# One fused H3-mixer and token-MLP kernel on one core: seven filler matmuls fewer before the last inverse stage, ScalarE's gelu table loaded after the inverse evictions, and new due times for its planner

## The chip, the core and the metric

The kernel runs on one core of one Trainium2 chip. The metric is the device time of one execution in microseconds (us). Below, PE is TensorE (matmuls; "PEld" its weight loads), DVE is VectorE, ACT is ScalarE, POOL is GpSimd, SP is SyncE, whose queue here only starts transfers.

## The reference

All inputs are bfloat16; the batch is 1, S = 2048 rows, D = 448 channels, F = 1792.

```python
x  = A_q
# mixer: short convolution of k, times v, long convolution by FFT, gate with the normed x
ks = sum over t of shift(k, t) * shift_k[:, t]          # 4 taps
kv = ks * v
y  = irfft(rfft(kv, 2S) * rfft(ssm_k, 2S))[:S] + kv * ssm_D
h  = x + layernorm(x) * y
# token MLP, over the rows
u  = gelu(einsum("sd,sf->df", layernorm(layernorm(h)), w1) + b1)   # tanh form
out = h + (einsum("df,fs->ds", u, w2) + b2).T
```

## The kernel before

The row index of every tensor is split as s = 16q + r, with q on the 128 partitions and r in 16 columns of tiles of 128 x 448 elements. All of SBUF is one tensor "arena" and all of PSUM is one tensor "ps" with 8 banks, so the profile knows only these two names and stages are told apart by line.

The convolution is a Fourier transform in two matmul stages with a transposing shuffle between them, done for the kernel (tag "k", with the filter) and for kv (tag "u"):

- **emit_tables** makes the sine tables and the small stage matrices, with Sin on ACT. It ends with a one-element gelu (line 793) whose only purpose is that its table load happens there.
- **emit_kv** (lines 868 to 890): DVE multiplies four shifted rows of k by the taps (879), PE adds them with an identity (885), DVE multiplies by v (888). **emit_kT** transposes the filter (914).
- **emit_stage1** (928 to 951), for k and then u: two matmuls for each r (933), an eviction by ACT alone (943), and two shuffle transfers, of 112 partitions from POOL and 16 from SP (947), into TK or TU. The evicted tile lies in a ring of 8 slots until both have landed. Every later tile needs all 16 shuffles of its tag.
- **emit_stage2** (956 to 971): four pairs of half-width matmuls (964) and an eviction by ACT or DVE for each of 16 tiles i. Tiles of k are scaled on the way out (653 on ACT, 656 on DVE), tiles of u are not (652, 655).
- **emit_ct** (973 to 1001): POOL copies (985, 990), PE transposes (996) and evictions make ET, the table of the last stage.
- **emit_products_i1** (1005 to 1055): DVE forms the products of a u tile and a k tile (1015), PE applies the first inverse stage (1027), ACT or DVE evicts in pairs, and shuffles go into TZ (1051; for the last pair 1040, from POOL, SP and ACT).
- **emit_warm** (1057 to 1062): matmuls whose result nobody reads, into one bank. N_WZ of them follow the last first-stage matmul; N_WI and N_WJ more lie inside the last inverse stage.
- **emit_q** (1072 to 1093): mean and variance of the rows of x, on DVE (1083, 1085) and POOL (1088, 1091).
- **emit_i2** (1102 to 1182): the last inverse stage, two matmuls for each r (1118), a gate by ACT with Identity (1125), the combination with x on DVE (1132), a sum of squares on ACT (1148) or bn_stats on DVE, small steps on POOL (1155 to 1167), and the normed row Q (1173).
- **emit_mlp** (1212 to 1250): the first layer for seven column blocks as rows of Q come (1218), gelu on ACT (1208), seven more blocks (1228), the second layer (1238), the final addition on DVE (1242), output on SP.

No order is written out by hand. Every operation is entered with a **due time** (`sch.t0`), its data dependencies, and a set of engines that may do it. `_Sched.schedule` then simulates the engines with estimated durations: an engine that is free takes, among the operations that are ready, the one with the smallest due time. Due times hold nothing back; they only rank what is ready at the same moment. An operation that ACT or DVE may do (most evictions) is passed over by DVE as long as ACT is due to be free within `flex_slack` ns, unless two or more operations are waiting for ACT (lines 329 to 332). The order found is emitted as one in-order stream for each engine, with semaphore waits where a dependency crosses engines.

The due times are set by constants on lines 639 to 645: T_U1 + T_DU1 r for stage 1 of u; T_K2 + T_D2 i and T_U2 + T_D2 i for stage 2 of k and of u; T_I1 + T_DI1 i for the products and first inverse stage; T_CT for ET's transposes; T_BIAS for a small transpose of b1; T_Q + T_DQ g for the statistics of rows 2g and 2g + 1; T_I2 + T_DI2 r for the last inverse stage, T_M1 + T_DI2 r for the MLP's first layer; and T_I2 - 50 for the N_WZ fillers.

Of the kernel before, what the change touches and what calls it, by code (L numbers as in the profile page):

```python
# [6 lines left out]
ACT = mybir.ActivationFunctionType  # L7
# [91 lines left out]
class _Sched:  # L99
# [48 lines left out]
    def op(self, W, fn, r=(), w=(), br=(), bw=(), n=0, kind=None, est=None, dmab=None, keng=16, rate=None, after=(), safter=()):  # L148
        o = _Op()
        o.id = len(self.ops)  # L150
        o.engs = W if isinstance(W, tuple) else (W,)
        o.eng = None
        o.fn = fn
        o.is_dma = dmab is not None
        o.nbytes = dmab or 0
        o.keng = keng
        o.lat = 2000.0 + o.nbytes / (22.0 * keng) if o.is_dma else 70.0
        if o.is_dma:
            o.est = {e: (600.0 if e != "pool" else 820.0) for e in o.engs}
        elif est is not None:  # L160
            o.est = dict(est) if isinstance(est, dict) else {e: est for e in o.engs}
        else:
            o.est = {e: self.est_of(e, n, kind) for e in o.engs}
        o.ev = None
        o.t0 = self.t0
        o.rate = rate or (18.0 if keng == 8 else 26.0)
        o.tag = self.tag
        o.acq = []
        o.bufs = []
        o.extra = []  # L170
        preds = set(after)
        spreds = set(safter)
        for spec in r:
            for c in self._cells(spec):
                preds.update(c.w)
                c.r.append(o.id)
        for spec in w:
            g = spec[2] if len(spec) > 2 else None
            for c in self._cells(spec):
                rd = [x for x in c.r if x != o.id]  # L180
                if g is not None and c.g == g and not rd:
                    preds.update(c.gb)
                    c.w.append(o.id)
                else:
                    base = rd if rd else list(c.w)
                    preds.update(base)
                    c.w = [o.id]
                    c.r = []
                    c.g = g
                    c.gb = base  # L190
        for b in br:
            if len(self.ops) and all(self.ops[x].engs == ("pe",) for x in b.writers):
                preds.add(b.writers[-1])
            else:
                preds.update(b.writers)
            b.readers.append(o.id)
            o.bufs.append(b)
            b.users.append(o.id)
        for b in bw:
            if not b.writers:  # L200
                o.acq.append(b)
            else:
                spreds.add(b.writers[-1])
            b.writers.append(o.id)
            o.bufs.append(b)
            b.users.append(o.id)
        preds.discard(o.id)
        spreds -= preds
        o.preds = sorted(preds)
        o.spreds = sorted(spreds)  # L210
        self.ops.append(o)
        return o.id
# [22 lines left out]
            return 300.0 + 0.9 * n  # L235
        return 450.0

    flex_slack = 600.0
    flex_back = 2

    def backlog(self, ready, ops, started, ready_t, t):
# [268 lines left out]
def _build(nc, A_q, A_k, A_v, A_shift_k, A_ssm_k, A_ssm_D, B_w1, B_b1, B_w2, B_b2, out):  # L510
# [8 lines left out]
    R = 16  # L519
# [37 lines left out]
    o_JK = o_DR + 896  # L557
# [8 lines left out]
    with ctx:  # L566
        sch = _Sched(nc, ctx, n_dma_sems=112, small_off=SMALL)
# [63 lines left out]
        def Ppair(b):  # L631
            s0, s1 = b.slots
            return PS[:, s0:s1 + 1, 0:D]
# [3 lines left out]

        FX = ("act", "dve")
        T_KV, T_DKV, T_KT, T_K1, T_DK1, T_U1, T_DU1 = -37.75, 0.96, -26.42, -39.56, 0.44, 2.72, 0.9
        T_K2, T_U2, T_D2, T_CT, T_BIAS, T_I1, T_DI1 = 29.29, -14.6, 1.375, 22.37, 56.3, 7.01, 0.974  # L640
        T_Q, T_DQ, T_I2, T_DI2, T_M1, T_W1 = 83.98, 14.35, 85.76, 0.401, 102.98, 122.45

        T_TH, T_TN = -36.0, -30.0
        T_CP, T_XL, T_WB = 20.0, -35.53, 154.44
        N_WZ, N_WI, N_W0, N_WK, N_WJ = 34, 6, 9, 3, 8

        def evac(dst, src, w, b, n, scale=None, engs=FX, r=(), est=None):

# [8 lines left out]
            bs = [b] if b is not None else []  # L657
            return op(engs, fn, r=r, w=w, br=bs, n=n, kind="psum", est=est)


        def emit_tables():
            N8 = 8192.0
# [124 lines left out]
            for k, (dst, i) in enumerate(((FW, 0), (MA, 1), (MB, 1))):  # L787
# [2 lines left out]
                   r=[(o_sv + 512 * k, 512), (o_msk + 512 * i, 512)], w=[(o_BD + 256 * k, 256)], n=128, kind="1x")  # L790
            op("pool", lambda e, W: e.tensor_scalar(out=MN, in0=MA, scalar1=-1.0, scalar2=None, op0=ALU.mult),
               r=[(o_BD + 256, 256)], w=[(o_BD + 768, 256)], n=128)
            op("act", lambda e, W: e.activation(out=JK[:, 0:1], in_=bias[:, 1:2], func=ACT.Gelu_apprx_tanh),
               r=[(o_b + 4, 4), (o_sv, 4 * NB)], w=[(o_JK, 4)], n=1)

        r_E = lambda r: (o_E + 512 * r, 512)
        r_ET = lambda r: (o_ET + 512 * r, 512)
# [203 lines left out]
                     est={"act": 1020.0, "dve": 690.0})  # L1001

        i1_last = []

        def emit_products_i1():
            for jj in range(R // 2):
                ms = []
                for h in range(2):
                    i = 2 * jj + h
                    sch.t0 = T_I1 + T_DI1 * i  # L1010
                    m = _Buf(mring)
                    ms.append(m)
                    ru = (o_TU + i * 2 * DB, 2 * DB)
                    aft = [x for w in wbufs for x in w.readers] if i == 0 else [mfirst[0]]
                    op("dve", lambda e, W, m=m, i=i: e.tensor_tensor(  # L1015
                        out=MR(m.slots[0]).rearrange("p (x y) d -> p x y d", x=2),
                        in0=TU[:, i].unsqueeze(2).broadcast_to([128, 2, 2, D]),
                        in1=TK[:, i].unsqueeze(1).broadcast_to([128, 2, 2, D]), op=ALU.mult),
                       r=[ru, (o_TK + i * 2 * DB, 2 * DB)], bw=[m], n=4 * D, after=aft)
                    if i == 0:  # L1020
                        mfirst.append(len(sch.ops) - 1)
                bs = [_Buf(psum, 2) for _ in range(2)]
                for h in range(2):
                    for t, (tab, xy) in enumerate(((MA, 0), (MN, 3), (MB, 1), (MB, 2))):
                        for par in range(2):
                            P = slice(64 * par, 64 * par + 64)
                            k = op("pe", lambda e, W, b=bs[h], m=ms[h], par=par, t=t, tab=tab, xy=xy, P=P: e.matmul(  # L1027
                                Pb(b, par), tab[P, :], MR(m.slots[0])[P, xy, :], start=(t == 0), stop=(t == 3)),
                               r=r_iv, br=[ms[h]], bw=[bs[h]], n=D, est=D / 4.15)
                            i1_last.append(k)  # L1030
                    evac(lambda jj=jj, h=h: TU[:, 2 * jj:2 * jj + 2, h, :], lambda b=bs[h]: Ppair(b),
                         [(o_TU + (4 * jj + h) * DB, DB), (o_TU + (4 * jj + 2 + h) * DB, DB)], bs[h], 2 * D)
                if jj == R // 2 - 1:
                    for h in range(2):
                        for par in range(2):
                            j = 2 * jj + par
                            p0 = 64 * (j & 1) + 32 * ((j >> 1) & 1) + (j >> 2)
                            o_h = o_TU + (2 * j + h) * DB
                            for q_, a, b_, j0 in (("sp" if h and par else "pool", 0, 112, 0), ("act" if h else "sp", 112, 128, 14)):
                                k = op(q_, lambda e, W, j=j, h=h, p0=p0, a=a, b_=b_, j0=j0: e.dma_start(  # L1040
                                    TZ[p0:p0 + 29:4, j0:j0 + (b_ - a) // 8, h, :], TU[a:b_, j, h, :]),
                                       r=[(o_h, DB)], w=[(o_TZ + j0 * 2 * DB, (b_ - a) // 8 * 2 * DB, "zpool" if a == 0 else "zsp")],
                                       dmab=(b_ - a) * DB, keng=8)
                                if a == 0:
                                    shuf["zpool"] = k
                    continue
                for par in range(2):
                    j = 2 * jj + par
                    p0 = 64 * (j & 1) + 32 * ((j >> 1) & 1) + (j >> 2)
                    for q_, a, b_, j0 in (("pool", 0, 112, 0), ("sp", 112, 128, 14)):  # L1050
                        shuf["z" + q_ + str(j)] = shuf["z" + q_] = op(q_, lambda e, W, j=j, p0=p0, a=a, b_=b_, j0=j0: e.dma_start(  # L1051
                            TZ[p0:p0 + 29:4, j0:j0 + (b_ - a) // 8].rearrange("p r c d -> p r (c d)"),
                            TU[a:b_, j].rearrange("p c d -> p (c d)")),
                           r=[(o_TU + j * 2 * DB, 2 * DB)], w=[(o_TZ + j0 * 2 * DB, (b_ - a) // 8 * 2 * DB, "z" + q_)],
                           dmab=(b_ - a) * 2 * DB, keng=8)
# [44 lines left out]
        qs = view(o_qst, [R, 4], f32)  # L1100

        def emit_i2():
            sch.t0 = T_M1 + 30.0
            op("pool", lambda e, W: e.tensor_tensor(out=bm, in0=qs[:, :, 0], in1=b2c, op=ALU.add),
               r=[(o_qst, 256), (o_b2c, 64)], w=[(o_bm, 64)], n=16)
# [192 lines left out]
```

## Time and profile before

| | us |
|---|---|
| five runs | 188.37, 188.92, 191.35, 191.58, 191.84 |
| their median | 191.35 |
| the profiled execution | 188.37 |
| its span, first to last instruction | 186.6 |
| busy in the span: PE / DVE / ACT / POOL | 173.8 / 110.0 / 97.2 / 71.4 |
| matmuls of 1218, 1228, 1238 (MLP), summed | 23.0, 21.4, 42.5 |
| the 48 filler matmuls of 1061 | 9.6 |
| ACT table loads: line 699 and line 793 | 1.3 and 1.3 |

The profiled execution is the lowest of the five runs. Its span is divided into the front (tables, kv, stages 1 and 2, products), which ends with the last eviction of the first inverse stage at 82.0 us; the shuffles after it, until about 87.4; the last inverse stage, which overlaps the first layer of the MLP, until 120; and two stretches of MLP matmuls to the end. A line of a timeline gives start, duration, engine, line of the source, operation and the number of instructions that it merges; in brackets is how long the engine had been idle before and what ended that.

### The profile page before, as it was taken

The page shows a single profiled execution, that of the slowest core. Times are in us where ns is not written, and L with a number is a line of the kernel's source. Part 1 is how long each engine was busy: PE and PEld are TensorE (multiplying, and loading weights), DVE is VectorE, ACT ScalarE, POOL GpSimd, SP SyncE. Part 2 cuts the span into 40 slices and gives each one's busy share as a digit, 9 for nine tenths or more (in the row PEclk, how much of TensorE's full clock was granted, in tenths as well). Part 3 has the DMA queues.
Part 4 walks back from the last instruction along what each step waited for, and adds up shares of the span by engine and source line. Part 5 has one row for each costly group of instructions (what it writes and reads, how often), then busy time and mean ns, then how long its engine had stood idle before and what let it go on. Part 6 is the DMA issues. An engine that isn't in the chain of part 4 may idle for free.

```text
span 186.6 us, 2835 instructions
## 1 busy us (share of the span) xinstructions
PE 173.8 (93%) x1033; PEld 91.8 (49%) x1033; DVE 110.0 (59%) x181; ACT 97.2 (52%) x141; POOL 71.4 (38%) x177
## 2 busy tenths in 40 slices
PE   7998897898988989899989999999999999999993
PEld 2653342343432433245334545555557777777772
DVE  8877999787789999997979756000001122212221
ACT  3497989888889989951886483442121000000000
POOL 8946976699520044587278576000000000000000
PEclk9999999999999999999999999999999999999999
DMA  5999597778449916774999999800000100111111
GB/s 167 377 418 316 181 260 222 233 222 236 137 115 393 353 46 183 225 238 112 351 394 401 425 422 422 343 5 0 0 0 4 49 34 15 49 53 49 49 49 49
DMA packets 15893, 35.44 MB, mean 190 GB/s; under 512 B 3901, under 2 KB 10062, under 8 KB 15878
## 3 DMA queue, kind: packets, MB, share of 16 engines
q1 hardware_dynamic: 11222, 25.66, 36.7%
q0 software_dynamic: 4608, 9.56, 17.9%
q8 instruction: 8, 0.13, 0.3%
q14 instruction: 7, 0.06, 0.1%
q10 hardware_dynamic: 48, 0.03, 0.0%
HBM read 22.37 MB, written 1.84 MB: 130 GB/s over the span
## 4 chain that ended last, share of the span: by engine, by line
PE 78%; ACT 10%; DVE 7%; DMA 3%; issue 1%; ACTq 0%
PE ps L1238 23%; PE ps L1228 11%; PE ps L1218 10%; PE ps L1061 5%; PE ps L885 5%; PE ps L1027 5%; ACT arena L943 4%; ACT arena L652 4%; PE ps L964 4%; PE ps L1118 3%; DMA arena<-arena 3%; PE ps L914 3%; PE ps L904 3%; PE ps L933 3%; DVE arena L1015 2%
## 5 line engine op out<-in xcount | busy, mean ns | idle before, releaser
L1242 DVE SCALAR_TENSOR_TENSOR arena<-ps,arena 128x448 bf16<-128x448 f32 x16 | 10.9, 684 | 56.9 <-PE ps L1238 56.9
L1238 PE MATMUL ps<-arena 128*128 128x448 bf16 x224 | 42.5, 352 | 0.0
L1238 PEld LDWEIGHTS ps<-arena 128*128 128x128 bf16 x224 | 32.3, 144 | 10.1
L943 ACT CAST arena<-ps 128x896 bf16<-128x896 f32 x32 | 26.7, 931 | 3.6 <-PE ps L933 1.7
L652 ACT CAST arena<-ps 128x896 bf16<-128x896 f32 (+1 forms) x26 | 22.0, 909 | 2.6 <-PE ps L868 1.7
L1218 PE MATMUL ps<-arena 128*128 128x448 bf16 x112 | 23.0, 353 | 0.3 <-DVE arena L1173 0.2
L947 POOL DMA_DIRECT2D arena<-arena x32 | 19.2, 601 | 7.7 <-ACT arena L943 4.7
L1228 PE MATMUL ps<-arena 128*128 128x448 bf16 x112 | 21.4, 352 | 0.0
L1208 ACT ACTIVATE arena<-ps,arena 128x448 bf16<-128x448 f32 x14 | 8.2, 639 | 20.1 <-PE ps L1228 14.7
L879 DVE TENSOR_TENSOR arena<-arena 128x1792 bf16<-128x1792 bf16 x16 | 18.2, 1175 | 0.0
L964 PE MATMUL ps<-arena 128*64 128x448 bf16 x128 | 16.4, 361 | 1.8 <-ACT arena L652 1.0
L1125 ACT ACTIVATE arena<-ps,arena 128x448 f32<-128x448 f32 x16 | 11.2, 722 | 12.0 <-PE ps L1118 9.0
L933 PE MATMUL ps<-arena 128*128 128x448 bf16 x64 | 16.0, 355 | 1.3 <-ACT arena L943 1.3
L885 PE MATMUL ps<-arena 128*128 128x448 bf16 x64 | 14.5, 354 | 2.4 <-ACT arena L943 1.8
L1015 DVE TENSOR_TENSOR arena<-arena 128x1792 bf16<-128x1792 bf16 x16 | 16.4, 1082 | 0.0
L1218 PEld LDWEIGHTS ps<-arena 128*128 128x128 bf16 x112 | 10.9, 98 | 11.1 <-DVE arena L1173 1.3
L1051 POOL DMA_DIRECT2D arena<-arena x14 | 8.2, 588 | 20.8 <-PE ps L964 15.6
L1228 PEld LDWEIGHTS ps<-arena 128*128 128x128 bf16 x112 | 11.0, 98 | 10.2
L1027 PE MATMUL ps<-arena 64*128 64x448 bf16 x128 | 14.1, 351 | 1.3 <-DVE arena L1015 0.6
L1132 DVE SCALAR_TENSOR_TENSOR arena<-arena 128x448 f32<-128x448 bf16 x16 | 10.7, 676 | 4.4 <-ACT arena L1125 4.4
L655 DVE CAST arena<-ps 128x896 bf16<-128x896 f32 (+2 forms) x11 | 9.5, 874 | 2.7 <-PE ps L868 1.2
L964 PEld LDWEIGHTS ps<-arena 128*64 128x64 f16 x128 | 5.4, 108 | 11.5 <-ACT arena L652 4.6
(88 smaller groups left out, 200.2 us busy)
## 6 DMA issues: line engine op xcount, KB each, us to landing
arena<-arena POOLq DMA_DIRECT2D x46, 196.0 KB, 4.9
arena<-in_B_w_dram SPq DMA_DIRECT2D x8, 896.0 KB, 9.2
arena<-in_B_w_dram SPq DMA_DIRECT2D x2, 2048.0 KB, 17.8
arena<-in_B_w_dram SPq DMA_DIRECT2D x2, 1536.0 KB, 19.9
arena<-in_A_k_dram SPq DMA_DIRECT2D x4, 448.0 KB, 7.8
arena<-in_A_v_dram SPq DMA_DIRECT2D x4, 448.0 KB, 8.4
arena<-in_A_q_dram SPq DMA_DIRECT2D x4, 448.0 KB, 5.0
out_dram<-arena SPq DMA_DIRECT2D x7, 224.0 KB, 1.9
```

The source lines that it names most:

```text
L652: return e.copy(out=dst(), in_=src())
L879: op("dve", lambda e, W, T=T, i=i, r=r: e.tensor_tensor(out=T[:, i], in0=KH[:, r:r + 4, :], in1=WT, op=ALU.mult), r=[(o_KH + r * DB, 4 * D ...
L885: op("pe", lambda e, W, b=b, T=T, i=i, j=j: e.matmul(Pb(b, i), ID, T[:, i, j, :], start=(j == 0), stop=(j == 3)), r=[(o_ID, 256), (o + (i ...
L933: op("pe", lambda e, W, b=b, r=r, h=h, dl=dl: e.matmul(Pb(b, h), E[:, 2 * r + h, :], src[:, r, :], start=True, stop=not dl), r=[r_E(r), (o ...
L943: return e.copy(out=dst, in_=Ppair(b)) if W == "act" else e.tensor_copy(out=dst, in_=Ppair(b))
L947: shuf[tag + q_ + str(r)] = shuf[tag + q_] = op(q_, lambda e, W, w=w, p0=p0, a=a, b_=b_, j0=j0: e.dma_start(T[p0:p0 + 29:4, j0:j0 + (b_ - ...
L964: op("pe", lambda e, W, b=bs[h], h=h, j=j, c=c, par=par: e.matmul(PS[64 * par:64 * par + 64, b.slots[c], 0:D], FW[:, 64 * c:64 * c + 64], ...
L1015: op("dve", lambda e, W, m=m, i=i: e.tensor_tensor(out=MR(m.slots[0]).rearrange("p (x y) d -> p x y d", x=2), in0=TU[:, i].unsqueeze(2).br ...
L1027: k = op("pe", lambda e, W, b=bs[h], m=ms[h], par=par, t=t, tab=tab, xy=xy, P=P: e.matmul(Pb(b, par), tab[P, :], MR(m.slots[0])[P, xy, :], ...
L1218: op("pe", lambda e, W, r=r, fc=fc, b=bs[fc]: e.matmul(Pb(b), W1A[:, r, 128 * fc:128 * fc + 128], Q[:, r, :], start=(r == 0), stop=(r == R ...
L1228: op("pe", lambda e, W, r=r, fc=fc, b=b: e.matmul(Pb(b), W1B[:, r, 128 * (fc - n0):128 * (fc - n0) + 128], Q[:, r, :], start=(r == 0), sto ...
L1238: op("pe", lambda e, W, r=r, fc=fc, b=b: e.matmul(Pb(b), W2[fc // 7][:, fc % 7, r:S:R], G[:, fc, :], start=(fc == 0), stop=(fc == NFC - 1) ...
```

## The change

The last fillers go from 34 to 27 (N_WZ). The one-element gelu leaves the tables and is entered at the head of emit_i2, with due time T_I2 - 8; it now waits for the last matmul and for the last two evictions of the first inverse stage, and its estimate is 1500 ns in place of some 231. The planner's `flex_slack` goes from 600 to 800 ns, and nine constants of due times change. No other instruction is added or removed; what else differs in the streams is their order, and which of ACT and DVE does a flexible eviction.

```diff
-    flex_slack = 600.0
+    flex_slack = 800.0
...
-        T_K2, T_U2, T_D2, T_CT, T_BIAS, T_I1, T_DI1 = 29.29, -14.6, 1.375, 22.37, 56.3, 7.01, 0.974
-        T_Q, T_DQ, T_I2, T_DI2, T_M1, T_W1 = 83.98, 14.35, 85.76, 0.401, 102.98, 122.45
+        T_K2, T_U2, T_D2, T_CT, T_BIAS, T_I1, T_DI1 = 37.66, -20.88, 1.238, 44.69, 51.65, -8.07, 0.974
+        T_Q, T_DQ, T_I2, T_DI2, T_M1, T_W1 = 84.58, 17.938, 100.42, 0.401, 102.98, 122.45
...
-        N_WZ, N_WI, N_W0, N_WK, N_WJ = 34, 6, 9, 3, 8
+        N_WZ, N_WI, N_W0, N_WK, N_WJ = 27, 6, 9, 3, 8
...
-            op("act", lambda e, W: e.activation(out=JK[:, 0:1], in_=bias[:, 1:2], func=ACT.Gelu_apprx_tanh),
-               r=[(o_b + 4, 4), (o_sv, 4 * NB)], w=[(o_JK, 4)], n=1)
+            tb_.append((bias, o_b))
...
         i1_last = []
+        i1_ev = []
...
-                    evac(lambda jj=jj, h=h: TU[:, 2 * jj:2 * jj + 2, h, :], lambda b=bs[h]: Ppair(b),
+                    k = evac(lambda jj=jj, h=h: TU[:, 2 * jj:2 * jj + 2, h, :], lambda b=bs[h]: Ppair(b),
                          [(o_TU + (4 * jj + h) * DB, DB), (o_TU + (4 * jj + 2 + h) * DB, DB)], bs[h], 2 * D)
+                    if jj == R // 2 - 1:
+                        i1_ev.append(k)
...
         def emit_i2():
+            sch.t0 = T_I2 - 8.0
+            bias, o_b = tb_[0]
+            op("act", lambda e, W: e.activation(out=JK[:, 0:1], in_=bias[:, 1:2], func=ACT.Gelu_apprx_tanh),
+               r=[(o_b + 4, 4)], w=[(o_JK, 4)], est=1500.0, after=i1_last[-1:] + i1_ev)
```

More of the change, by code (lines that the diff above doesn't have):

```diff
@@ L658, in evac @@
             return op(engs, fn, r=r, w=w, br=bs, n=n, kind="psum", est=est)
+        tb_ = []
         def emit_tables():
```

## The prediction, made before the changed kernel was built or run

> **What bounds the kernel now.** I read first the page's table of the span in 40 slices (4.67 us each; the digit is the busy share in tenths):
>
> ```profile
> PE   7998897898988989899989999999999999999993
> DVE  8877999787789999997979756000001122212221
> ACT  3497989888889989951886483442121000000000
> PEclk9999999999999999999999999999999999999999
> ```
>
> From slice 25 on only PE is full, at full clock. Up to slice 17 no engine is free: ACT and DVE share the evictions and are both full. The chain of waits gives the tail: MLP matmuls run without a gap from 112.00 to 183.69, and the change touches none of them. So the time is the moment at which the last inverse stage (line 1118) can start, plus some 99 us behind it (186.6 - 87.6).
>
> What sets that moment is read from the busy time by stretch (start:end and length, then busy us of PE, PEld, DVE, ACT and POOL, each with its number of instructions):
>
> ```profile
> 50.10:55.00 4.90, 4.41 (x42) 1.72 (x39) 4.09 (x4) 4.39 (x6) 2.15 (x9) 1.00 0.34 98
> 55.00:63.00 8.00, 6.93 (x60) 2.27 (x61) 7.14 (x8) 7.66 (x10) 0.00 (x0) 1.00 1.01 367
> 63.00:82.00 19.00, 17.36 (x157) 6.98 (x154) 18.32 (x23) 17.73 (x21) 8.70 (x15) 1.00 0.62 184
> 82.00:87.50 5.50, 5.50 (x31) 2.84 (x29) 5.37 (x17) 0.00 (x0) 5.34 (x13) 1.00 0.58 169
> ```
>
> From 55 to 82 ACT is busy 25.4 of 27.0 us and DVE 25.5: evictions and products bound this part, not PE. In the 5.5 us after it ACT does no work at all. Then the moved table load, in the timelines of ACT, PE and DVE:
>
> ```profile
> 25.78 4.24 ACT L943 CAST arena<-ps 128x896 bf16<-128x896 f32 x5 [0.23 <-PE ps L933]
> 30.04 1.28 ACT L793 ACT_TABLE_LOAD   x1
> 31.33 0.21 ACT L793 ACTIVATE arena<-arena 128x1 bf16<-128x1 f32 x1
> 31.44 3.31 ACT L943 CAST arena<-ps 128x896 bf16<-128x896 f32 x4
> 35.24 4.95 ACT L943 CAST arena<-ps 128x896 bf16<-128x896 f32 x6 [0.50 <-DMA arena<-arena]
> ...
> 32.38 0.93 PE L885 MATMUL ps<-arena 128*128 128x448 bf16 x4 [1.03 <-ACT arena L943]
> ...
> 35.15 1.09 DVE L888 TENSOR_TENSOR arena<-ps,arena 128x896 bf16<-128x896 f32 x1 [1.05 <-PE ps L885]
> ```
>
> The load sits between two evictions. PE then waits 1.03 us for a bank that the next eviction frees, and DVE 1.05 us for PE. Last, the fillers, in the chain and in SP's timeline:
>
> ```profile
> 81.12 6.61 PE ps L1061 x34
> 87.72 1.53 PE ps L1118 x8
> ...
> 87.35 0.93 SPq L1192 DMA_DIRECT2D arena<-in_B_w_dram  x2
> ```
>
> SP's weight load (1192) waits for the last shuffle and goes at 87.35; the first matmul of 1118 is recorded at 87.56. Fillers and shuffles end together.
>
> **What the Trainium skill says.** "ScalarE: Activation LUTs", section "What ACT_TABLE_LOAD costs": 1283 ns for the load, some 1380 ns more for a drain. The trace has the same 1283 ns, but only 1.40 us from its start to the next eviction (30.04 to 31.44), so I use 1.40. The same page, "Table sets: the hidden batching unit": copy and identity are in every set. The trace agrees for plain copies under the Sin set (line 943 from 15.64 on) and for Identity and Square under gelu's; the scaled Copy (653) has so far run only under gelu's. "TensorE: Matmul & The Clock Gate", "What's actually happening": the clock halves after an idle window of about 3.4 us. The longest PE gap here that nothing covers, 1.03 us, left the clock full.
>
> **The change part by part.**
>
> *Table load out of the front.* One load and one activation, 1.40 us of ACT at 30 us. Smallest gain 0.5: the chain runs through a shuffle landing at 35.15, whose slot the eviction at 35.24 wants, so ACT could wait there instead. Largest 1.4. DVE's kv chain (879, 888) is what stage 1 of u waits for until 48, and it gets its 1.05 us back whatever the slot does. I take **-1.2**, the middle of 1.05 and 1.40.
>
> *Table load behind the evictions.* It waits for the last two evictions, ended at 82.00. ACT's queue has two shuffle issues then (1040, until 83.99; their due time 6.5 is ahead of the load's 92.4), then the load, done at 85.4. Behind it stand the gates of 1118, first at 88.14. Cover 2.7 us, cost **0**. If the load came ahead of the two issues, their tiles would land 1.4 later: upper end +1.4. A reload for the scaled Copy or for Identity would show as 1.28 us each; the section quoted excludes it.
>
> *Fillers.* 34 take 6.61 us, 194 ns each; 27 take 5.25 and end at 86.4. The shuffles still land at 87.35, so PE then idles about 1.0 us and 1118 starts at 87.4 in place of 87.56: **-0.2**, and nothing if the transfers set both. The gap is under the window above. Were the clock halved for one window, the loss would be at most 1.7 (half of 3.4), an estimate from the clock page.
>
> *Due times and flex_slack.* Two orders change that matter.
> (a) Before, tiles of u in stage 2 ranked -14.6 to 6.0, all ahead of the products (from 7.0). Now product i (-8.07 + 0.974 i) passes stage-2 tile i' once i' > 10.3 + 0.79 i. DVE's products start before the last five u tiles, and with flex_slack at 800 DVE takes fewer of those. From 55 to 82 there are 36 flexible evictions (16 u, 16 inverse, 4 k), one of ET, and 16 products. ACT's row "54.99 6.59 x8" gives 0.82 us each, DVE's "60.09 3.07 x3" 1.02, its products "67.51 6.09 x6" 1.015. With 7 on DVE, as now, DVE has 23.4 us of work between 55.95 and 79.99, and the tail behind it (matmuls 0.97, two evictions) ends at 82.0. With 5 on DVE it has 21.3, ACT 26.4 of 27. Gain up to 1.5, ACT then binding.
> (b) ET (due 44.7, was 22.4) now ranks behind the first six k tiles in place of ahead of all. Between 40 and 50 ACT has 2.1 us of gaps (0.60, 0.33, 0.62, 0.58). Freed ACT time there, with ET's 1.0 at 46.79 put off, takes up to four k tiles that now come after 68; four evictions of 0.82 over two engines are up to 1.7.
> The upper end of gain is 3.2. Nothing forces it; a list order can also lose, see below. I take **-2.2**, two thirds, because both move work from the engine that ends last into gaps that the trace shows.
>
> *The last inverse stage.* From row 7 on, MLP rows up to r - 6.4 now rank ahead of row r of 1118. Before, rows 7 to 15 took 94.34 to 111.4 with MLP rows in between; nine MLP rows of 7 x 0.19 and nine of 0.38 are 15.4, no more. PE is full there either way. The last Q row is ready at 114.5 and is wanted at 117.4 (120.1 less 14 x 0.19): 2.9 us of cover. Cost 0, between -0.5 (a gap of 0.44 less) and +1.5. T_Q, T_DQ and T_BIAS leave the ranking of what matters as it was: 0.
>
> Sum: -1.2 - 2.2 - 0.2 = -3.6. Against the profiled execution, 188.37 (span 186.6 and 1.77 around it), that is 184.8. It is the lowest of five, 2.98 under the median; against the median, **187.7**.
>
> **Rivals.**
> 1. *Only the load counts.* The new order moves work about in a stretch that stays full, and order brings between +1 and -1. For it: 55 to 82 is already 94% busy on both engines. Sum -1.2 - 0.2: 190.0.
> 2. *k tiles starve (slower).* Stage 2 of k is now last of all (37.7 to 56.2) while both its rivals moved ahead; products need a k tile each. Before, 12 of 16 were done by 55. If 8 or more are left there, that is four more evictions on full engines (about 3.7) and, for each of those late pairs, one wait of DVE for four matmuls (0.57) and an eviction (0.92): 4 x 1.5 = 6 at most, taken as 2.5. With the load's gain: 191.35 + 3.7 + 2.5 - 1.4 = 196.2. It decides from three late tiles more than now. Against it: before 55 nothing but ET competes with k tiles, and ET moved back.
> 3. *The load lands on the path.* It delays ACT's shuffle issues or the first gate: +1.4 takes back the gain. 189.4 or, with no gain from order, 191.4. Against it: due times and 2.7 us of cover.
>
> **How the numbers follow.** Forecast 0.60, its range 184.9 to 190.2 (order from -3.2 to 0, load -0.5 to -1.4, 1.5 for a median taken among runs that spread by 3.5); rival 1: 0.18; rival 3: 0.05; rival 2: 0.17. Two per cent is 3.8 us, about what a measurement of this kernel can tell from no change; the forecast lies just on that line. I put 0.45 of its 0.60 beyond it, since the runs fall both near 188.5 and near 191.5 and a shift that empties the upper group counts in full. So faster 0.45, same 0.15 + 0.18 + 0.05 = 0.38, slower 0.17. Range 184.2 to 192.3: it takes in rivals 1 and 3 and leaves out rival 2 and a little below.
>
> **What would show it.** Right: no table load near 30 and the waits of 1.03 and 1.05 gone; the load at 84 to 85.5 with nobody waiting for it; last eviction near 78.5; PE idle about 1 us between 27 fillers and 1118, clock at 1.00; from 1118 to the end 99 us as before. Wrong: evictions of 653 or 656 crowded after 60 with DVE's products waiting for them; or fewer than 99 us from 1118 to the end, which would put the gain where I see none.

## The result and the profile after

The change makes the kernel a little slower. Median before 189.81 us over 80 runs beside it (187.98 to 192.84), after 191.71 over 43 (189.07 to 195.25); the ratio after/before is **1.0062 [1.0039, 1.0084]**, some 1.2 us, where 1.9% less was forecast. Ratios here leave out disturbed executions, which the medians contain, so a ratio can differ from the quotient of its medians.

The profiled execution took 191.28 us, with a span of 189.5 (before: 188.37 and 186.6). Before's is near the lowest of its runs, so these two lie further apart (2.9 us) than the medians' 1.9 or the ratio. Lines moved by 1 to 8: 1118 is now 1126, 1061 is 1065, 1051 and 1040 are 1055 and 1044, 943 is 944, 1015 is 1017; the table load of 793 is now at 1109.

The page's table of 40 slices of after, its PE row and granted clock:

```profile
PE   7998899999888998892979999999999999999993
...
PEclk9999999999999999999699999999999999999999
```

Two things are new: the 19th slice with PE at 2 tenths, and in the one behind it a clock of 6 tenths. The busy time by stretch (columns as in the prediction; the decimal after POOL is the granted clock, then the DMA share and GB/s), first after, then before:

```profile
85.00:88.80 3.80, 0.00 (x0) 0.00 (x1) 0.44 (x1) 0.30 (x2) 1.33 (x3) 1.00 0.22 72
88.80:93.40 4.60, 4.51 (x15) 1.78 (x16) 3.24 (x9) 2.57 (x4) 0.09 (x1) 0.63 0.79 254
...
88.83:189.50 100.67, 96.00 (x494) 58.51 (x494) 33.05 (x79) 27.61 (x58) 18.44 (x44) 0.98 0.38 147
```

```profile
87.56:186.60 99.04, 94.87 (x495) 57.76 (x493) 32.40 (x78) 27.48 (x58) 17.43 (x45) 1.00 0.38 149
```

PE does nothing for 3.8 us, and the 4.6 us after it run at 0.63 of the clock. The last two rows split the 2.9 us of span: the last inverse stage starts 1.27 later (88.83 for 87.56) and takes 1.63 more from there to the end (100.67 for 99.04). The trace's clock record shows the dip as one stretch of 3.41 us at half clock, beginning at 89.8.

The chain of waits of after (start, us, what):

```profile
85.00 3.63 DMA arena<-arena
88.63 0.20 issue
88.83 2.27 PE ps L1126 x8
91.10 0.05 issue
91.14 2.30 PE ps L1065 x6
```

The fillers no longer reach the shuffles: they end at 85.00, and the chain runs through a transfer. It is SP's last shuffle, which was issued at 85.00 and landed last of all, at 88.63 (before: issued at 82.89, landed at 87.33). The eight matmuls of 1126 took 1.68 us before, the six fillers 1.31. ACT's timeline of after:

```profile
33.40 1.71 ACT L944 CAST arena<-ps 128x896 bf16<-128x896 f32 x2 [0.32 <-DMA arena<-arena]
35.45 3.33 ACT L944 CAST arena<-ps 128x896 bf16<-128x896 f32 x4 [0.34 <-DMA arena<-arena]
39.50 1.71 ACT L944 CAST arena<-ps 128x896 bf16<-128x896 f32 x2 [0.72 <-DMA arena<-arena]
...
83.81 1.28 ACT L1109 ACT_TABLE_LOAD   x1 [3.22 <-issue]
...
89.41 2.57 ACT L1133 ACTIVATE arena<-ps,arena 128x448 f32<-128x448 f32 x4 [4.09 <-PE ps L1126]
```

The load is where it was meant to be, and the first gate (1133) waits for PE, not for it. But where the load used to stand, ACT now stops three times for a slot of the ring (1.4 us, before 0.5 in one wait).

Last the shuffles of the first inverse stage: timelines of POOL and SP, first after, then before. A duration on SP or POOL is the time to issue, not to land.

```profile
68.59 4.65 POOL L1055 DMA_DIRECT2D arena<-arena  x8 [17.60 <-PE ps L855]
...
63.31 19.56 SPq L1055 DMA_DIRECT2D arena<-arena  x14
82.91 2.78 SPq L1044 DMA_DIRECT2D arena<-arena  x3
88.65 1.22 SPq L1200 DMA_DIRECT2D arena<-in_B_w_dram  x2
```

```profile
68.09 2.33 POOL L1051 DMA_DIRECT2D arena<-arena  x4 [15.62 <-PE ps L964]
...
66.28 15.12 SPq L1051 DMA_DIRECT2D arena<-arena  x14
81.46 2.16 SPq L1040 DMA_DIRECT2D arena<-arena  x3
```

SP's row of 14 contains its waits, so its start is what counts: 3.0 us earlier (63.31 for 66.28), while POOL's first burst comes half a microsecond later. POOL therefore opens with eight queued transfers in place of four. From 71 us on, seven of SP's issues take 1.0 to 1.8 us in place of 0.67, so its last one goes out 4.4 us behind the last eviction; before it was 0.9. SP's weight load, which waits for the last shuffle, goes at 88.65 in place of 87.35, although the last eviction ended at 80.60 in place of 82.00. What held POOL until 68.6 is the subject of half of the experiments.

### The profile page after: what moved, and what is told of

Same layout as the page of the kernel before. It is cut to its first block, busy times and chain, and to the rows that moved or that the text cites. A ratio compares the mean times of both kernels' runs of the same rounds, so it can differ in the third digit from the quotient of the medians.

```text
span 189.5 us, 2816 instructions
## 1 busy us (share of the span) xinstructions
PE 172.5 (91%) x1026; PEld 91.8 (48%) x1026; DVE 108.9 (57%) x180; ACT 96.9 (51%) x142; POOL 72.2 (38%) x177
## 4 chain that ended last, share of the span: by engine, by line
PE 69%; DMA 13%; ACT 8%; DVE 5%; ACTq 2%; issue 2%; SPq 1%
PE ps L1246 22%; PE ps L1226 11%; PE ps L1236 11%; DMA arena<-arena 10%; PE ps L1029 5%; PE ps L1126 4%; PE ps L965 4%; ACT arena L652 3%; PE ps L886 3%; DMA arena<-in_A_ssm_k_dram 3%; ACT arena L944 2%; PE ps L1065 2%; PE ps L915 2%; ACTq L1044 2%; PE ps L934 2%
## 5 line engine op out<-in xcount | busy, mean ns | idle before, releaser
L1246 PE MATMUL ps<-arena 128*128 128x448 bf16 x224 | 42.5, 352 | 0.0
L652 ACT CAST arena<-ps 128x896 bf16<-128x896 f32 (+2 forms) x27 | 21.9, 888 | 3.1 <-PE ps L869 2.0
L1226 PE MATMUL ps<-arena 128*128 128x448 bf16 x112 | 22.7, 352 | 0.0
L1236 PE MATMUL ps<-arena 128*128 128x448 bf16 x112 | 21.4, 352 | 0.0
L934 PE MATMUL ps<-arena 128*128 128x448 bf16 x64 | 16.2, 355 | 1.8 <-ACT arena L944 1.7
L965 PE MATMUL ps<-arena 128*64 128x448 bf16 x128 | 15.6, 360 | 2.0 <-ACT arena L652 0.7
L1236 PEld LDWEIGHTS ps<-arena 128*128 128x128 bf16 x112 | 11.0, 98 | 10.2
L886 PE MATMUL ps<-arena 128*128 128x448 bf16 x64 | 14.5, 354 | 1.0 <-ACT arena L944 0.8
L1126 PE MATMUL ps<-arena 128*128 128x448 bf16 x32 | 8.8, 376 | 5.5 <-DMA arena<-arena 3.8
L655 DVE CAST arena<-ps 128x896 bf16<-128x896 f32 (+1 forms) x10 | 9.5, 947 | 2.8 <-PE ps L869 1.2
```

Source lines behind the costliest of these rows:

```text
L652: return e.copy(out=dst(), in_=src())
L886: op("pe", lambda e, W, b=b, T=T, i=i, j=j: e.matmul(Pb(b, i), ID, T[:, i, j, :], start=(j == 0), stop=(j == 3)), r=[(o_ID, 256), (o + (i ...
L934: op("pe", lambda e, W, b=b, r=r, h=h, dl=dl: e.matmul(Pb(b, h), E[:, 2 * r + h, :], src[:, r, :], start=True, stop=not dl), r=[r_E(r), (o ...
L965: op("pe", lambda e, W, b=bs[h], h=h, j=j, c=c, par=par: e.matmul(PS[64 * par:64 * par + 64, b.slots[c], 0:D], FW[:, 64 * c:64 * c + 64], ...
L1226: op("pe", lambda e, W, r=r, fc=fc, b=bs[fc]: e.matmul(Pb(b), W1A[:, r, 128 * fc:128 * fc + 128], Q[:, r, :], start=(r == 0), stop=(r == R ...
L1236: op("pe", lambda e, W, r=r, fc=fc, b=b: e.matmul(Pb(b), W1B[:, r, 128 * (fc - n0):128 * (fc - n0) + 128], Q[:, r, :], start=(r == 0), sto ...
```

## The experiments

**Theories.** *A (clock):* 27 fillers leave PE idle so long that the clock halves. *B (shuffles):* POOL's shuffles wait for the last transpose of ET, which ends at 68.29. (The profile names line 855, a single transpose of b1 that PE runs right behind it.) The copies that ET's transposes read lie at `o_TT + 16384` and on, and `o_TT = o_TZ`: they occupy part of TZ, into which the shuffles write. SP's part lies outside. *C (load):* the moved load is what costs. *D (k tiles):* the new order starves the products of k tiles. The diffs are cut to the lines that matter ("..."); each starts from the kernel that its heading names.

**e1 and e8: after with 34 fillers again** (the same kernel twice).

```diff
-        N_WZ, N_WI, N_W0, N_WK, N_WJ = 27, 6, 9, 3, 8
+        N_WZ, N_WI, N_W0, N_WK, N_WJ = 34, 6, 9, 3, 8
```

> The changed kernel with 34 fillers after the first inverse stage instead of 27. Theory (late shuffles, then a cold clock): the shuffles still land near 88.6 us, because nothing in this edit touches them; but the fillers then end near 86.3, PE idles 2.3 us instead of 3.8, the clock stays at 1.00, and the first eight matmuls of the last stage take 1.5 instead of 2.3 us and the six fillers after them 1.2 instead of 2.3. The time falls by 1.5 to 2 us against the changed kernel and is then within 1 us of the kernel before. Rival (the new order of the last inverse stage costs the time, not the clock): the granted clock goes to 1.00 but the stretch from the last stage's start to the end stays near 100.7 us and the time falls by under 0.5.

e1: four runs of 189.8 to 193.6, too few for a ratio; profile at full clock, start to end 98.54. It was repeated:

> The changed kernel with 34 fillers once more, to have it timed: its first look gave few runs. Theory: the clock is 1.00 in nearly all runs, where it was below in most runs of the changed kernel, and the time lies 1 to 2 us under the changed kernel's, at the one before or up to 0.5 per cent above it, since the shuffles still land 7 to 8 us after the last eviction. Rival (the clock is a by-product): clocks of 1.00, and the time as that of the changed kernel, 0.5 to 0.8 per cent above the one before.

e8: 0.9963 [0.9903, 1.0023]; in the profile clock 1.00, 98.5 from start to end, last stage still late (88.92). A fits, but the planner had used the larger planned total to reorder the last stage too, so this isn't one part alone. e9 keeps that order.

**e9: after with 34 fillers, everything else in its place.** Each filler's estimate is cut so that 34 are planned as long as 27 were.

```diff
-        N_WZ, N_WI, N_W0, N_WK, N_WJ = 27, 6, 9, 3, 8
+        N_WZ, N_WI, N_W0, N_WK, N_WJ = 34, 6, 9, 3, 8
...
-                   r=r_fw + [(o_ET, 2 * D)], bw=[b], n=D, after=after() if i == 0 else ())
+                   r=r_fw + [(o_ET, 2 * D)], bw=[b], n=D, after=after() if i == 0 else (), est=150.88235294117646 if n_ == N_WZ else None)
```

> The changed kernel with 34 fillers, each entered with an estimate of 151 ns in place of 190, so that the planner sees the same total and every other instruction on every engine stands where the changed kernel has it. Only seven dead matmuls are added. Theory (the clock): shuffles land near 88.6 us or 8 us after the last eviction as in the changed kernel, PE's gap before the last stage is 2.3 us instead of 3.8, the clock is 1.00 in nearly all runs, from the first matmul of the last stage to the end it takes 98.7 to 99.2 us instead of 100.7, and the time is 0.7 to 1.0 per cent below the changed kernel's, at ratio 0.997 to 1.000 to the one before. Rival (it was the order that 34 planned fillers give the last stage, as eight rows in a regular alternation, not the clock): the clock goes to 1.00 but the time stays at a ratio of 1.004 to 1.008.

1.0001 [0.9962, 1.0041]. Its PE timeline, and its stretch from the start of the last stage to the end:

```profile
81.47 6.61 PE L1065 MATMUL ps<-arena 128*128 128x448 f16 x34
89.39 1.67 PE L1126 MATMUL ps<-arena 128*128 128x448 bf16 x8 [1.31 <-DMA arena<-arena]
```

```profile
89.39:188.50 99.11, 94.43 (x494) 58.13 (x494) 32.80 (x79) 27.76 (x58) 18.67 (x44) 1.00 0.39 149
```

Seven dead matmuls are added, every other instruction stands where it stood, and the end comes 1.56 us sooner after the start (99.11 for 100.67): the gap is 1.31 and the clock holds. The two ratios, 1.0062 and 1.0001, point the same way, with intervals that overlap by a hair.

Single executions say the same. One stretch of 3.41 us at half clock lowers the mean clock of a span of 189.5 us to 0.991. A mean of 0.989 to 0.991 stands in 17 of the 44 executions of after whose clock is on record, and in one of 196 of before. Of the 23 in after's ratio, the eight at full clock took 189.07 to 189.89 us (mean 189.5), the eleven with this mark 189.78 to 191.74 (mean 190.9): 1.4 us for the dip in one and the same kernel. The executions of before in the ratios below have medians of 188.9 to 189.4. So **A is shown**, and the dip makes up most of the loss.

Two limits remain. With 34 fillers the mark became rarer but did not go, although a full clock in nearly all executions was expected (e8: 4 of 20, e9: 5 of 22). And lower means, 0.97 to 0.98, occur in before too (47 of 196): in the profiles of e4, e5 and e14 the clock was halved for 6.8 or 10.2 us from 13.3 to 13.8 on, long before the fillers. No run tests why.

**e5 and e10: before with 27 fillers**, first plainly, then with estimates that keep the order (239 ns each).

```diff
-        N_WZ, N_WI, N_W0, N_WK, N_WJ = 34, 6, 9, 3, 8
+        N_WZ, N_WI, N_W0, N_WK, N_WJ = 27, 6, 9, 3, 8
...
```

> The kernel before with 27 instead of 34 fillers after the first inverse stage; nothing else. Theory (the shuffles set the start of the last stage; the clock falls only where the gap gets long): the shuffles land near 87.4 us as before, PE idles about 1.0 us between fillers and last stage, the clock stays at 1.00 and the time is within 0.3 per cent of the kernel before. Rival (the shorter filler run alone lets the clock fall): the clock reads 0.98 to 0.99, the first matmuls of the last stage take twice as long, and the time rises by 1 to 2 us.

> The kernel before with 27 fillers, each entered with an estimate of 239 ns, so that the planned total and with it every other instruction's place are those of before. Only seven dead matmuls are taken out. Theory (in the kernel before the gap of about 1.0 us is too short for the clock, and what made the earlier kernel with 27 fillers slower was the new order that the planner gave the last stage): clock 1.00 as before, the last stage starts at or up to 0.2 us before 87.56, ratio 0.997 to 1.002. Rival (27 fillers alone let the clock fall or start the last stage later): clock 0.98 to 0.99 in most runs and a ratio of 1.007 to 1.012, as in the earlier kernel.

e5 1.0092 [1.0057, 1.0126], e10 0.9988 [0.9952, 1.0024]: the same seven matmuls fewer, 0.9% slower or no difference. e10's PE timeline:

```profile
80.80 5.28 PE L1061 MATMUL ps<-arena 128*128 128x448 f16 x27
88.37 1.68 PE L1118 MATMUL ps<-arena 128*128 128x448 bf16 x8 [2.29 <-DMA arena<-arena]
```

A gap of 2.29 leaves the clock alone (start to end 99.03). Behind e5's gap of 1.91 the clock was full too, yet it took 100.69 to the end. The planner, told of a shorter filler run, had reordered the last stage, and PE now stood still for ACT's gates four times (0.63 three times, 0.82 once) where before waits twice (0.44 and 0.42). So removing fillers costs nothing on before's timing, and changing their number can cost through the plan, which wasn't expected.

**e2, e7, e11: after with ET early**: T_CT is −25.0 in e2, and 2.0 in e7 and e11, which are one kernel.

```diff
-        T_K2, T_U2, T_D2, T_CT, T_BIAS, T_I1, T_DI1 = 37.66, -20.88, 1.238, 44.69, 51.65, -8.07, 0.974
+        T_K2, T_U2, T_D2, T_CT, T_BIAS, T_I1, T_DI1 = 37.66, -20.88, 1.238, 2.0, 51.65, -8.07, 0.974
```

> The changed kernel with the due time of ET's transposes at -25 instead of 44.69, so that they rank ahead of stage 2 of u; all else as changed. Theory (POOL's shuffle transfers wait for ET's last transposes, since the copies these read lie where the transfers write[...]): POOL's first transfer goes near 63.5 instead of 68.6 us, SP's issues fall back from 1.5 to 0.7 us, the shuffles land 4 to 5 us after the last eviction, near 85.5 instead of 88.6, PE's gap is under 1 us, the clock is 1.00, and the time is 3 to 5 us below the changed kernel, 1 to 2 below the one before. Rival (ACT's two shuffle issues and the table load behind them hold the last tiles up): the landing stays at 8 us after the last eviction and the time moves by under 1 us.

> The changed kernel with ET's due time at 2.0 instead of 44.69: ahead of stage 1 of u by a hair and of stage 2 of k, but behind stage 2 of u; in the planned order ET's last transposes stand ahead of the first product matmul. 27 fillers. Theory: ET's last transpose near 53, POOL's first transfer within 1 us of the first eviction of the first inverse stage, SP's issues at 0.7 us, the last shuffle lands 4.5 to 5.5 us after the last eviction (8.0 in the changed kernel), PE's gap is under 1 us and the clock 1.00. If the front keeps the changed kernel's end (last eviction near 81) the time is 2 to 3 us below the changed kernel and 1 to 2 below the one before; if k tiles come late, with DVE waiting for them as in the last experiments, the front ends near 82.5 to 83 and the time equals that of before. Rival (ET has nothing to do with it): landing stays at 8 us after the last eviction.

> The changed kernel with ET's due time at 2.0 once more, to have it timed: its first look gave four runs, one of them the shortest of all. Theory: as in that look, last shuffle 4.5 to 5.5 us after the last eviction, PE's gap under 1 us, clock 1.00; the time is 1.0 to 1.5 per cent below the changed kernel and at a ratio of 0.990 to 0.996 to the one before. Rival (that look was luck with the transfers): ratio 0.998 to 1.004.

e2: 0.9993 [0.9963, 1.0023], some 1.3 us below after where 3 to 5 were expected; ET's last transpose ends at 53.2 in place of 68.3, and POOL's first shuffle goes at 65.74, right behind its eviction. e7: four runs (186.4, 189.6, 190.7, 191.2), repeated as e11: **0.9939 [0.9908, 0.9970]**, below before and below after's ratio. Timelines of POOL and SP in e11:

```profile
66.07 1.17 POOL L1055 DMA_DIRECT2D arena<-arena  x2 [14.68 <-ACT arena L652]
...
65.80 15.23 SPq L1055 DMA_DIRECT2D arena<-arena  x14
81.08 2.13 SPq L1044 DMA_DIRECT2D arena<-arena  x3
86.61 0.93 SPq L1200 DMA_DIRECT2D arena<-in_B_w_dram  x2
```

POOL now follows ACT's evictions two by two, and the last stage starts at 86.69, with 27 fillers, a gap of 0.93 and a full clock.

**e3: after with three of the four copies in KT's memory**, ET left late.

```diff
-                oc = o_cp + 2048 * h
+                oc = o_cp if h == 0 else o_KT + 2048 * (h - 1)
```

> The changed kernel with three of the four copies that ET's transposes read laid into memory that stage 1 of k has freed, so that no transfer of the first inverse stage waits for a transpose; due times as changed. Theory of the shared memory: POOL's first transfer goes within 1 us of the first eviction of the first inverse stage (near 64 instead of 68.6), the last shuffle lands near 85.5 instead of 88.6, the last stage starts there, and the time is 3 to 4 us below the changed kernel, even though ET's transposes stay late. Rival (the transfers are late because ET itself is late, by the load on PE or ACT, not by memory): little moves, under 1 us. Rival (ACT's issues): landing stays 8 us after the last eviction.

0.9977 [0.9942, 1.0012]. ET's last transpose still comes at 69.4, but POOL's timeline begins

```profile
64.69 1.17 POOL L1055 DMA_DIRECT2D arena<-arena  x2 [11.06 <-ACT arena L652]
```

4.7 us ahead of ET's end. It is the shared memory that held POOL, not ET's lateness as such: **B is shown**. The ratio falls from 1.0062 to 0.9977, some 1.6 us where 3 to 4 were expected: in the profile the transfers take 2.6 us less behind the last eviction, but that eviction comes as much later, since this kernel's products stood still for late k tiles (70.7 to 73.9). Its gap is 1.27, at full clock.

How long the transfers take behind the last eviction goes with POOL's first burst, though the rows for four and two overlap:

| POOL's first burst | last eviction to first matmul of the last stage, us |
|---|---|
| eight (after, e1, e8, e9) | 8.2, 7.3, 7.5, 7.0 |
| four (before, e5, e10) | 5.6, 6.3, 6.7 |
| two (e2, e3, e4, e7, e11, e12, e13, e14) | 4.5, 5.7, 5.9, 5.1, 5.3, 5.1, 5.8, 6.0 |

e6, with ten and 6.6, stands outside: there the products had stopped meanwhile. What sets the first row apart is SP's last shuffle, the last to land. It goes out 3.8 to 4.4 us behind the last eviction in the four profiles of that row, and 0.5 to 1.3 in those of the other two.

**e4: after with the load early again; e6: before with the load late.**

> The changed kernel with the one-element gelu back at the end of the tables; fillers and due times as changed. Theory of the late shuffles: the load takes ACT 1.4 us near 30 again, PE and DVE wait some 1 us each there, the last eviction of the first inverse stage is some 0.5 to 1.4 us later than 80.6, but the shuffles, held by ET's transposes and their queue, land within 1 us of 88.6 as before; PE's gap is shorter by what the front lost, so the clock may hold, and the time is the same or up to 1.5 us lower. Rival (the moved load holds up ACT's shuffle issues): ACT's two issues take 0.7 to 1.2 us each again instead of 1.5 and 1.6, the shuffles land near 86 and the time falls by 2.5 or more. My forecast's own reading (the load's place is worth 1.2 us): the time rises by 1.2.

> The kernel before with the one-element gelu moved behind the evictions of the first inverse stage, as in the change; 34 fillers and the due times of before. With the load out of its way the planner's own order also changes: ET's last transposes come after 64 of the 128 matmuls of the first inverse stage's first half instead of after 40, and the products run in blocks. Theory: ACT gets 1.4 us back near 30, the waits of PE and DVE of 1.0 there are gone, and the last eviction comes 0.5 to 1.4 us before 82.0; but POOL's transfers still wait for ET, so the shuffles land no earlier than 87 and the time is within 1 us of before. Rival (the table load behind the evictions delays ACT's shuffle issues or the first gate): the load's end and the first gate are less than 0.2 us apart, or ACT's issues take over 1.4 us each, and the time rises by 1 us or more. My forecast's reading: the time falls by 1.2.

e4 1.0064 [1.0028, 1.0100], e6 1.0218 [1.0140, 1.0297] (four runs). Neither is clean: the planner laid out another order each time. e4 did ET at 56, and in its profile the halved clock of the front (from 13.8) comes on top; e6 left six k tiles until 75 to 79. DVE's timeline of e6:

```profile
66.71 6.22 DVE L1017 TENSOR_TENSOR arena<-arena 128x1792 bf16<-128x1792 bf16 x6
...
75.30 2.19 DVE L656 TENSOR_SCALAR arena<-ps 128x896 bf16<-128x896 f32 x2 [0.42 <-PE ps L965]
77.40 6.09 DVE L1017 TENSOR_TENSOR arena<-arena 128x1792 bf16<-128x1792 bf16 x6
```

Products end at 72.9 and go on at 77.4. Theory D, the prediction's slower rival, is thus a real case of this planner, but with before's due times; after itself has 12 of 16 k tiles done by 55, as before.

**e12, e13, e14: the load's place with all else fixed.** e12 and e14 are e11 with 30 fillers in e11's order; e13 adds the early gelu with an estimate that moves nothing, so that the table is loaded at 29.9 and again nowhere later.

```diff
...
+            op("act", lambda e, W: e.activation(out=JK[:, 0:1], in_=bias[:, 1:2], func=ACT.Gelu_apprx_tanh),
+               r=[(o_b + 4, 4), (o_sv, 4 * NB)], w=[(o_JK, 4)], est=1.0)
...
```

> As the one with ET's due time at 2.0, with 30 fillers in place of 27, whose estimates keep the planned total and the order. Theory: the three more fill what is left of PE's gap (27 ended at 84.8 and the last stage began at 85.5), so the runs whose clock fell go away and the time is the same or up to 0.3 per cent lower than with 27. Rival (30 reach past the landing): the last stage starts up to 0.6 us later and the time rises by as much.

> The kernel with ET's due time at 2.0 and 30 fillers, with a one-element gelu at the end of the tables as in the kernel before, entered with an estimate of 1 ns so that every other instruction stands where it stood; the load now happens there, between the same two evictions as in the kernel before, and the one-element gelu behind the inverse evictions stays and finds its table loaded. Only the load's place differs from the next run. My forecast's reading (1.2 us, between 0.5 and 1.4): near 30 us PE waits about 1.0 us for a bank and DVE about 1.0 for PE; the last eviction comes 0.9 to 1.4 us later, and the ratio is 0.005 to 0.007 above the next run's. Rival (ACT waits in that stretch for ring slots that shuffles have not left yet, and the load only fills that wait): ACT's waits for transfers between 30 and 40 us shrink by as much as the load takes, the last eviction moves by under 0.4 us, and the two ratios agree within 0.003.

> The kernel with ET's due time at 2.0 and 30 fillers once more, as the pair of the run above and to have it timed with more runs. Theory: ratio 0.988 to 0.994 to the kernel before; clock 1.00 in nearly all runs; last stage starting 4.5 to 5.5 us after the last eviction. Rival (the six runs of the first look were a lucky draw): ratio 0.996 or above.

e12 0.9894 [0.9834, 0.9955] (six runs), e13 0.9954 [0.9918, 0.9990], e14 0.9973 [0.9944, 1.0002]. e14 repeats e12, so e12's six runs were a lucky draw, as the rival had it. With the load early, the waits of PE and DVE come back in e13's profile (1.04 and 1.25 us near 32 and 35). But the last operation of the kv chain starts 31.2 us after stage 1's first eviction in e13, and 29.6, 32.0 and 30.2 us after it in e11, e12 and e14, without the early load: what the waits cost is lost in the spread. In the times there is no gain from moving it: e13 lies between the two timings of the kernel without it. C, a cost of the late load, finds no support either.

## Why the prediction was wrong, step by step

The prediction's sum was −1.2 for the load, −2.2 for the due times and −0.2 for the fillers. Between the two profiled executions the last eviction came 1.4 earlier, the way from there to the last stage took 2.7 more, and the last stage to the end 1.6 more: +2.9 in all. Two terms failed, the fillers and the due times, and one cost was left out, ET's.

- **Fillers: the step that turned a gain into a loss.** "The shuffles still land at 87.35, so PE then idles about 1.0 us" and "the gap is under the window above". The gap was 3.83 us, and −0.2 became +1.6. The price was there (1.7 for one window; e9 gives 1.56), and so was the number it hangs on. "TensorE: Matmul & The Clock Gate", section "What's actually happening", puts the idle window at about 3.4 us: gaps of 1.31, 1.91 and 2.29 left the clock full here and 3.83 halved it, which agrees. What was missing was to carry the prediction's own −3.4 of the front into this step: with fillers ending that much earlier and shuffles fixed at 87.35 the gap would have come to over 4 us. Both can't be had: either the shuffles move with the front, or the gap opens.
- **Due times (a) and (b): the largest term, −2.2, came to nothing.** From DVE's first product to the last eviction it took 25.05 us in all four profiles of after's order (after, e1, e8, e9) and 24.92 in all three of before's (before, e5, e10). The lines of DVE and ACT at its two ends, first after, then before:

```profile
55.55 1.09 DVE L1017 TENSOR_TENSOR arena<-arena 128x1792 bf16<-128x1792 bf16 x1
...
78.75 1.85 ACT L652 CAST arena<-ps 128x896 bf16<-128x896 f32 x2 [0.20 <-PE ps L1029]
```

```profile
57.08 1.09 DVE L1015 TENSOR_TENSOR arena<-arena 128x1792 bf16<-128x1792 bf16 x1
...
80.15 1.85 ACT L652 CAST arena<-ps 128x896 bf16<-128x896 f32 x2 [0.15 <-PE ps L1027]
```

DVE still did seven of the flexible evictions, the one ahead of its first product included, where (a) had five, and the four k tiles of (b) did not come earlier: 12 of 16 by 55 in both. The last eviction's 1.4 us were gained ahead of the first product. That part isn't steady: after's order began its first product at 55.55, 57.14, 56.39 and 57.30, before's at 57.08 and 56.76 (e5 later, behind its halved clock).
- **ET put off (b): its cost left out.** It was counted only as ACT time freed. Nobody asked who waits for the memory of its copies. ET's end hardly moved (67.8 to 68.3), but the shuffles behind it were wanted 3 us earlier, and the way from last eviction to last stage took 2.7 us more in the two profiles, 1.3 on the averages of the table's first two rows. e11 and e3 take this wait away in two ways.
- **Load out of the front: mechanism right, size not shown.** The waits of 1.03 and 1.05 went, and the last operation of the kv chain began 1.3 earlier (46.46 to 45.17). The lower bound's reason also came true: ACT waited for ring slots instead, 1.4 us for 0.5. In the times e13 and e14 show no gain, where −1.2 was taken; a gain below some 0.4% stays open.
- **Load behind the evictions: right.** Done at 85.09, gate at 89.41, nobody waiting; no second load for the scaled Copy.
- **Last inverse stage: right** once the clock is held: 99.11 in e9 for 99.04.
- **Rivals and range.** No rival hit: the loss that came was an upper end of the forecast's own step, not a case. "Only the load counts" was right to give the order of the front nothing, and wrong on the fillers. That after's median of 191.71 lies inside the range of 184.2 to 192.3 is luck: the range was built on a median of five runs, 191.35, and 80 runs gave 189.81. Nor does the forecast's own upper end of 190.2 follow from the terms it names: 191.35 − 0.5 − 0.2 + 1.5 is 192.2.

What stays open: why executions of one order reach the first product up to 1.8 us apart; why a longer burst on POOL slows SP's issues; and how much of e11's gain over before (0.6%, where e14 with three fillers more shows 0.3%) is due to ET and how much to the other due times.

## What to carry to other kernels

When dead matmuls bridge a gap, the gap has two ends: work out again how long it is whenever the work ahead gets shorter or the transfer it waits for gets later, and compare that sum with the longest gap known to be harmless. When an operation is put off, look for who writes into its inputs' memory, since a buffer laid over another makes a wait that no data flow shows. Where a planner orders the code, test one part with estimates chosen so that the order stays; the plan that came with a changed number of fillers cost 0.9% here.

## What the runs showed of the hardware

- After an idle gap of 3.83 us PE's clock fell to half for one stretch of 3.41 us, which began at 89.8, 0.9 us after work had resumed. Not every execution of this kernel shows it: 17 of 44 have the mean clock that one such stretch leaves, and ten a full one.
- The clock was also halved early in some executions, for 6.8 us (e4) or 10.2 us (e5, e14) from 13.3 to 13.8 on; half or more of the executions of each of these kernels show a full clock.
- SP mostly took longer to issue its transfers where POOL's queue had been long. Its last three shuffles (1044) took 2.8 us in after, 3.7, 3.7 and 3.4 in e1, e8 and e9, where POOL began with eight. Where it began with two they took 2.1 to 2.3 (e2, e3, e7, e11, e12, e13), with 2.7 and 2.8 in e4 and e14 as exceptions; with four 2.2 to 2.9, and with ten (e6) 2.6. Whether the backlog is the cause wasn't tried.
